# Fetching the chosen rows of one batch by one-hot matmuls from SBUF, in a kernel whose work order a planner writes

## The chip, the cores and the metric

The kernel runs on one core of a Trainium2 chip. The metric is the device time of one launch in microseconds (us), the median of several runs. The profiled execution is one more run, with its own time and a span from the first to the last instruction.

## What is computed

Two parts follow each other. For each of 4 batches, q, k and v are 6208 × 256. An attention across the 256 channels is formed from all 6208 rows, and then 128 rows of its output go through a small two-layer network.

```python
qn = q / (np.linalg.norm(q, axis=1, keepdims=True) + 1e-06)
kn = k / (np.linalg.norm(k, axis=1, keepdims=True) + 1e-06)
s = kn.transpose(0, 2, 1) @ qn / tau
a = softmax(s)                      # 256 x 256 per batch
x = v @ a                           # 6208 x 256 per batch
scores = np.einsum('bsd,d->bs', x, w_gate)
for b in range(4):
    top_idx = the 128 rows with the highest scores[b]
    xe = x[b, top_idx]
    ye = np.maximum(xe @ w1, 0.0) @ w2
    out[b] = x[b]; out[b, top_idx] = xe + sigmoid(scores[b, top_idx])[:, None] * ye
```

## The kernel before

**Tiles.** Each batch is cut into six chunks of 1024 rows and a rest of 64. A chunk lies in SBUF as 128 partitions of 8 rows, so column c of a batch (49 of them) is 128 rows, one to a partition. Loads are issued by POOL (L187, L189) and turn float32 into bfloat16 on the way: first q and k of a batch, then its v. Five buffers hold chunks of q, five of k, five of v; a buffer's next load waits until TensorE has read the old chunk.

**Stages of a batch.** `p1_row` (L292 on) multiplies each row of q and k into the sums of k'q and the squares (L303, L305, L307). `softmax_stages` makes a from them: norms on VectorE, one small matmul (L350), the exponentials (L357, ScalarE), the vector aw = a·w_gate, and a in bfloat16 (L376). `p2_transpose` turns four columns of v at a time on TensorE (L403) into a PSUM bank, and ScalarE (L417) or VectorE (L419) copies them to SBUF as vt_sb; eleven such places exist, and those of batch 3 lie in freed q and k buffers. There are two banks named vt_ps for this, and at the very end also s_ps and g_ps. `p2_score` multiplies turned groups by aw (L440). `p2_out` multiplies two columns at a time by a (L474), here called an output group, and ScalarE evicts each into a stage of float32 (L482), from which SP stores whole chunks (L514).

**Selection.** `select_stages` finds the 128 highest scores: the maxima of each partition are spread over all partitions by a matmul (L544), seven rounds narrow a threshold (compare on VectorE, L557; count on TensorE, L573, and VectorE, L576), then the chosen positions are packed into an index (L587 to L622). POOL gathers the chosen rows of v by an indirect DMA (L626), TensorE turns them (L637), and the attention and the two layers follow (L645 to L689). The result, upd, is scattered over the stored rows by a second indirect DMA from POOL (L721), which waits for the batch's stores. Both DMAs stand in POOL's one queue, between loads.

**Order.** A planner writes the order of every engine when the program is built: at each step it takes the ready piece of work with the best rank, by its own clocks for each engine and a model of the two DMA rings (`Rings`). Its waiting TensorE is kept busy with dead matmuls (`idle`, L865). The number of places for turned groups (`VT_BUFS`) and of load buffers (`V_BUFS`) enters its choices: `in_use`, `limit` and `vt_live` say when a load or a transposition may be placed. So a change of either number changes the order in all batches. Stores of batch 2 and 3 are held back behind the last loads, and two chunks of batch 1 are stored last of all, with their chosen rows already added.

Of the kernel before, what the change touches and what calls it, by code (L numbers as in the profile page):

```python
# [10 lines left out]
F32 = mybir.dt.float32  # L11
BF16 = mybir.dt.bfloat16
# [3 lines left out]
ALU = mybir.AluOpType  # L16
AX = mybir.AxisListType

P = 128
RPP = 8  # L20
CHUNK = RPP * P
NTHR = 8
# [5 lines left out]
def kernel(  # L28
# [12 lines left out]
    nc = tc.nc  # L41

    B, N, C = q.shape
# [7 lines left out]
    NFULL = N // CHUNK  # L51
    REM = N - NFULL * CHUNK
    assert 0 < REM <= P
    NCOL = NFULL * RPP + 1
    inv_tau = 1.0 / float(tau)

    QK_BUFS = 5
    V_BUFS = 5
    ST_BUFS = 9
    VT_BUFS = 11  # L60
    AHEAD = 4

    const = ctx.enter_context(tc.tile_pool(name="const", bufs=1))
# [7 lines left out]
    moe = ctx.enter_context(tc.tile_pool(name="moe", bufs=1))  # L71
# [4 lines left out]
    ps_vt = ctx.enter_context(tc.tile_pool(name="ps_vt", bufs=2, space=PS))  # L76
    ps_o = ctx.enter_context(tc.tile_pool(name="ps_o", bufs=2, space=PS))
    ps_sc = ctx.enter_context(tc.tile_pool(name="ps_sc", bufs=1, space=PS))
    ps_m = ctx.enter_context(tc.tile_pool(name="ps_m", bufs=1, space=PS))
# [3 lines left out]
    v_flat = v.rearrange("b n c -> (b n) c")  # L83
# [65 lines left out]
    rings = Rings()  # L149
    vt_clock = {"pe": 0.8, "dve": 0.8, "act": 0.8, "pool": 0.8, "sp": 0.8}  # L150

    def now():
        return vt_clock["pe"]
# [8 lines left out]
    loaded = {}  # L162
    load_inst = {}
    arrival_key = {}
    in_use = {"qk": 0, "v": 0, "qkr": 0, "vr": 0}
# [3 lines left out]
    dmas = []  # L169
# [94 lines left out]
    for i in range(NSTEP):  # L264
        nc.vector.memset(pows[:, i, :], 1.00001 / (NTHR + 1) ** (i + 1))
    jpows = const.tile([P, NSTEP, NTHR], F32)
    nc.vector.tensor_tensor(out=jpows, in0=pows,
                            in1=iota_row[:, None, 1:NTHR + 1].to_broadcast([P, NSTEP, NTHR]), op=ALU.mult)
    ones_col = const.tile([P, NCOL], BF16)
    nc.vector.memset(ones_col, 1.0)  # L270
    cnt9 = const.tile([P, NTHR + 1], F32)
# [234 lines left out]
    def emit_store(b, ci, parts):  # L506
# [12 lines left out]
        keep.extend(ins)  # L519
        return ins[0]  # L520

    def select_stages(b):
        sc_ps = sc_tiles[b]
        sc = moe.tile([P, NCOL + 1], F32, name="sc")
# [28 lines left out]
        nc.vector.tensor_scalar(out=tab, in0=jpows, scalar1=rng, scalar2=None, op0=ALU.mult)  # L553
        wait = 1.8
        for i in range(NSTEP):
            cmp = moe.tile([P, NCOL, NTHR], BF16, name="cmp", bufs=2)
            nc.vector.scalar_tensor_tensor(out=cmp, in0=sc[:, 0:NCOL, None].to_broadcast([P, NCOL, NTHR]),  # L557
                                           scalar=wl[:, i, NTHR:NTHR + 1],
                                           in1=tab[:, None, i, :].to_broadcast([P, NCOL, NTHR]),
                                           op0=ALU.subtract, op1=ALU.is_ge)  # L560
            if i == 0:
                nc.vector.tensor_scalar(out=wl[:, 0:NSTEP, 0:NTHR], in0=pows, scalar1=rng, scalar2=None,
                                        op0=ALU.mult)
            if i == 1:
                nc.vector.scalar_tensor_tensor(out=slack, in0=wl[:, 0, NTHR:NTHR + 1], scalar=-1.0, in1=top,
                                               op0=ALU.mult, op1=ALU.max)
                nc.vector.tensor_scalar(out=slack, in0=slack, scalar1=-5.0e-7,
                                        scalar2=wl[:, NSTEP - 1, 0:1], op0=ALU.mult, op1=ALU.subtract)
            yield ("pe", 0.2 if i else 0.5, wait, "slot" if i > 1 else "")
            wait = 1.2  # L570
            mps = ps_m.tile([P, 512], F32, name="m_ps")
            for h in range(7):
                nc.tensor.matmul(mps[:, 0:7 * NTHR], lhsT=ones_b,  # L573
                                 rhs=cmp[:, 7 * h:7 * h + 7, :].rearrange("p s j -> p (s j)"),
                                 start=h == 0, stop=h == 6)
            nc.vector.tensor_reduce(out=cnt9[:, 0:NTHR],  # L576
                                    in_=mps[:, 0:7 * NTHR].rearrange("p (s j) -> p j s", s=7),
                                    axis=AX.X, op=ALU.add)
            gej = moe.tile([P, NTHR + 1], F32, name="gej", bufs=2)
            nc.vector.scalar_tensor_tensor(out=gej, in0=cnt9, scalar=float(CAP) - 0.5, in1=wl[:, i, :],  # L580
                                           op0=ALU.is_ge, op1=ALU.mult,
                                           accum_out=wl[:, i + 1, NTHR:NTHR + 1])
# [16 lines left out]
        nc.tensor.matmul(sc_ps[:, 0, 0:1], lhsT=tri_b[:, 0, :], rhs=own_b, start=True, stop=True)  # L599
        excl_b = moe.tile([P, NCOL + 1], BF16, name="excl_b")  # L600
        nc.scalar.copy(excl_b, sc_ps[:, 0, 0:1].to_broadcast([P, NCOL + 1]))
        oh = moe.tile([P, P], BF16, name="oh")
        nc.vector.tensor_scalar(out=oh, in0=iota_row, scalar1=mps[:, 0:1], scalar2=None, op0=ALU.is_ge)
        nc.vector.scalar_tensor_tensor(out=oh, in0=iota_row, scalar=mps[:, 1:2], in1=oh, op0=ALU.is_lt,
# [13 lines left out]
        if b == late[0][0]:  # L618
# [2 lines left out]
        idx = moe.tile([P, 1], I32, name="idx", bufs=2)  # L621
        nc.vector.tensor_scalar(out=idx, in0=tok, scalar1=float(N - 1), scalar2=float(b * N), op0=ALU.min,  # L622
                                op1=ALU.add)
        yield ("pool", 0.15, 0.9)
        vg = moe.tile([P, C], BF16, name="vg", bufs=2)
        ins = nc.gpsimd.indirect_dma_start(out=vg, out_offset=None, in_=v_flat,  # L626
                                     in_offset=bass.IndirectOffsetOnAxis(ap=idx[:, 0:1], axis=0))
        dmas.append(ins)
        vt_clock["pool"] = max(vt_clock["pool"], now()) + 1.0
        rings.add(0, vt_clock["pool"] + 1.0, 0.5, ("gather", b))  # L630
        gathered.add(b)

        yield ("dma", ("gather", b))
        a_sb, _ = a_tiles[b]
        tp = ps_vt.tile([P, 2, 4, P], BF16, name="vt_ps")
        for cc in range(2):
            nc.tensor.transpose(tp[:, cc, 0, :], in_=vg[:, cc * P:(cc + 1) * P], identity=ident_b)  # L637
        vgt = moe.tile([P, 2, P], BF16, name="vgt")
        nc.vector.tensor_copy(vgt, tp[:, :, 0, :])
        yield ("pe", 0.12, 0.3)  # L640

        xt_ps = ps_vt.tile([P, 2, C], F32, name="vt_ps")
        for dc in range(2):
# [88 lines left out]
    def calm():  # L732

        if acc_dead[0]:
            return L in gathered
        if softmaxes[0]:
            return False
        near = eat[eat_at:eat_at + 14]
        return not any(x[0] == "T" for x in near) or near[0][0] == "T"

    class Chain:
# [33 lines left out]
        def ready(self):  # L775
            if self.need[0] == "t":
                if self.b == E and self.mlp and acc_dead[0] and L not in gathered:
                    return FAR
                return self.need[1]
            if self.need[0] == "dma":  # L780
                if self.b < L and not calm() or self.b == L and out_at < len(outs):
                    return FAR

                late_by = vt_clock["pool"] + 3.8 if self.b == L else 0.0
                return max(rings.landing(self.need[1]) + 0.1, late_by)
            b = self.need[1]
            if self.need[0] == "scores":
                return now() if score_at == len(scores) else FAR
            if held[b] or (b >= E and L not in gathered):
                return FAR  # L790
            if b >= E:
                return now()
            return max(rings.landing(key) for key in stored[b]) + 3.0
# [73 lines left out]
    while True:  # L867
# [106 lines left out]
        elif what == "T":  # L974
# [20 lines left out]
            vt_bank = sorted(vt_bank)[1:] + [fin]  # L995
            vt_live = len(from_pool)
            vt_ready[(u[1], g)] = fin
            if eat_at == len(eat) or eat[eat_at][1] != u:
                in_use[bucket(u)] -= 1
        elif what == "S":  # L1000
            b, g = scores[score_at]
# [61 lines left out]
```

## Time and profile before

| | |
|---|---|
| median of 3 runs | 258.37 us (258.06 to 258.6) |
| profiled execution | 257.8 us |
| its span | 255.8 us |
| TensorE busy | 214.7 us (84%) |
| VectorE busy | 92.6 us (36%) |
| ScalarE busy | 106.4 us (42%) |
| POOL busy | 56.9 us (22%) |
| granted TensorE clock, mean | 0.977 |
| read from and written to HBM | 78.91 MB and 25.95 MB |

Times in the profile count from the start of the span. A row of a timeline gives the start, the duration, the engine, the line and the operation, and in square brackets how long its engine had been idle and what released it. PE is TensorE, DVE is VectorE, ACT is ScalarE. A digit of a slice is the busy share in tenths. DMA shares can pass 1 since packets on one engine overlap.

### The profile page before, as it was taken

What the parts mean: (1) busy time and instruction counts of PE and PEld (TensorE: products, weight loads), DVE (VectorE), ACT (ScalarE), POOL (GpSimd) and SP (SyncE); (2) the same over time, 40 slices, a digit from 0 to 9 for tenths busy, and PEclk for the clock granted to TensorE, in tenths of its full rate; (3) what the DMA queues carried; (4) which work ended last, traced back from release to release, by engine and by line L of the source; (5) the groups of instructions that cost most, each with busy time, mean ns of one, the idle gap of its engine ahead of it and who ended that gap; (6) DMA issues with size and microseconds to landing.
All of it is one profiled execution on the core that took longest, in us unless ns stands there. A gap on an engine that the chain in (4) does not pass through costs nothing.

```text
span 255.8 us, 6666 instructions
## 1 busy us (share of the span) xinstructions
PE 214.7 (84%) x2878; PEld 187.9 (73%) x2878; DVE 92.6 (36%) x410; ACT 106.4 (42%) x187; POOL 56.9 (22%) x106
## 2 busy tenths in 40 slices
PE   0099779899998529989999689899999999999962
PEld 0069768798877529879888578788898878887851
DVE  2000002635651003445655006546752064687021
ACT  2800003753564002484244005765313069698740
POOL 7323111422005000622200414212313310000301
PEclk9999999999999959999999999999999999999987
DMA  6999999999999999999999999999999999999995
GB/s 235 259 216 215 213 216 210 215 209 251 274 320 314 316 285 216 218 214 213 249 282 258 213 211 213 215 261 316 220 215 218 212 225 225 407 425 411 404 415 250
DMA packets 17326, 66.87 MB, mean 261 GB/s; under 512 B 2097, under 2 KB 3634, under 8 KB 14450
## 3 DMA queue, kind: packets, MB, share of 16 engines
q0 software_dynamic: 12672, 38.93, 76.5%
q1 hardware_dynamic: 4626, 27.53, 26.7%
q8 instruction: 22, 0.36, 0.5%
q14 instruction: 6, 0.05, 0.0%
HBM read 78.91 MB, written 25.95 MB: 410 GB/s over the span
## 4 chain that ended last, share of the span: by engine, by line
DMA 73%; PE 14%; issue 4%; POOL 4%; DVE 2%; ACT 1%; POOLq 1%; DVEq 0%
DMA k_ch<-in_k_dram 48%; DMA v_ch<-in_v_dram 10%; DMA q_ch<-in_q_dram 10%; DMA out_dram<-stage 4%; PE s_ps L303 2%; PE o_ps L474 2%; PE vt_ps L403 2%; POOL q_ch L187 1%; PE g_ps L307 1%; PE g_ps L305 1%; ACT stage L482 1%; PE s_ps L474 1%; PE sc_ps L440 1%; PE g_ps L474 1%; POOL k_ch L187 1%
## 5 line engine op out<-in xcount | busy, mean ns | idle before, releaser
L303 PE MATMUL s_ps<-q_ch,k_ch 128*128 128x256 bf16 x384 | 90.0, 279 | 28.7 <-DMA k_ch<-in_k_dram 28.7
L305 PE MATMUL g_ps<-q_ch 128*128 128x128 bf16 x384 | 85.5, 223 | 0.0
L307 PE MATMUL g_ps<-k_ch 128*128 128x128 bf16 x384 | 85.5, 223 | 0.0
L482 ACT COPY stage<-o_ps 128x512 f32<-128x512 f32 x77 | 43.9, 589 | 43.6 <-PE o_ps L474 41.6
L303 PEld LDWEIGHTS <-k_ch 128*128 128x128 bf16 x384 | 38.3, 100 | 31.5 <-DMA k_ch<-in_k_dram 30.6
L307 PEld LDWEIGHTS <-k_ch 128*128 128x128 bf16 x384 | 38.3, 100 | 5.2
L305 PEld LDWEIGHTS <-q_ch 128*128 128x128 bf16 x384 | 38.3, 100 | 0.1
L474 PE MATMUL o_ps<-a_sb,vt_sb 128*128 128x256 bf16 (+1 forms) x250 | 35.5, 272 | 1.0 <-ACT stage L482 0.5
L317 DVE CUSTOM_DVE_ANT_0 junk<-g_ps,ident_f 128x128 f32<-128x128 f32 x16 | 4.7, 291 | 66.4 <-PE g_ps L307 66.0
L474 PEld LDWEIGHTS <-vt_sb 128*128 128x128 bf16 (+1 forms) x264 | 23.6, 97 | 6.4 <-issue 3.1
L403 PE MATMUL vt_ps<-ident_b,v_ch 128*128 128x128 bf16 x360 | 25.4, 219 | 2.7 <-ACT vt_sb L417 2.4
L403 PEld LDWEIGHTS <-v_ch 128*128 128x128 bf16 x384 | 23.1, 97 | 5.1 <-issue 3.4
L313 ACT COPY s_sb<-s_ps 128x512 f32<-128x512 f32 x4 | 2.3, 586 | 55.4 <-PE s_ps L303 55.4
L187 POOL DMA_DIRECT2D v_ch<-in_v_dram x26 | 14.2, 545 | 45.8 <-PE vt_ps L403 17.5
L417 ACT COPY vt_sb<-vt_ps 128x1024 bf16<-128x1024 bf16 (+1 forms) x26 | 22.6, 927 | 2.9 <-PE vt_ps L403 2.9
L187 POOL DMA_DIRECT2D q_ch<-in_q_dram x25 | 13.8, 554 | 29.9 <-DMA q_ch<-in_q_dram 10.4
L187 POOL DMA_DIRECT2D k_ch<-in_k_dram x25 | 13.6, 543 | 24.5 <-DMA v_ch<-in_v_dram 10.4
L865 PE MATMUL o_ps<-w_sb,ident_b 128*128 128x256 bf16 x124 | 18.8, 273 | 0.2 <-ACT h_sb L675 0.2
L557 DVE SCALAR_TENSOR_TENSOR cmp<-sc,wl,tab 128x392 bf16<-128x392 f32 x28 | 17.5, 627 | 1.0
L626 POOL DMA_INDIRECT vg<-in_v_dram,idx x4 | 4.0, 1008 | 61.0 <-DVE idx L622 32.8
L865 PEld LDWEIGHTS <-ident_b 128*128 128x128 bf16 x124 | 10.7, 97 | 1.3 <-issue 0.4
L576 DVE TENSOR_REDUCE cnt<-m_ps 128x8 f32<-128x56 f32 x28 | 6.0, 216 | 15.3 <-PE m_ps L573 14.9
(188 smaller groups left out, 273.7 us busy)
## 6 DMA issues: line engine op xcount, KB each, us to landing
out_dram<-stage SPq DMA_DIRECT2D x21, 1024.0 KB, 10.2
q_ch<-in_q_dram POOLq DMA_DIRECT2D x23, 512.0 KB, 17.8
k_ch<-in_k_dram POOLq DMA_DIRECT2D x23, 512.0 KB, 18.5
v_ch<-in_v_dram POOLq DMA_DIRECT2D x22, 512.0 KB, 14.2
stage<-in_moe_w_dram SPq DMA_DIRECT2D x2, 1024.0 KB
out_dram<-stage SPq DMA_DIRECT2D x4, 512.0 KB
v_ch<-in_v_dram POOLq DMA_DIRECT2D x4, 256.0 KB, 12.9
out_dram<-stage SPq DMA_DIRECT2D x2, 384.0 KB, 5.0
```

What stands on the lines that cost most here:

```text
L187: ins = nc.gpsimd.dma_start(out=t[:, rows, :], in_=view(src, b, ci)[:, rows, :])
L303: nc.tensor.matmul(s_ps[:, cc, :], lhsT=ks[:, sl], rhs=qs, start=begin and cc == 0, stop=end and cc == 1)
L305: nc.tensor.matmul(g_ps[:, cc, :], lhsT=qs[:, sl], rhs=qs[:, sl], start=begin and cc == 0, stop=False)
L307: nc.tensor.matmul(g_ps[:, 2 + cc, :], lhsT=ks[:, sl], rhs=ks[:, sl], start=False, stop=end and cc == 1)
L317: nc.vector.tensor_tensor_reduce(out=junk, in0=g_ps[:, i, :], in1=ident_f, scale=1.0, scalar=0.0, op0=ALU.mult, op1=ALU.add, accum_out=nsq ...
L403: nc.tensor.transpose(vt_ps[:, cc, j, :parts], in_=vt[:parts, s0 + j, cc * P:(cc + 1) * P], identity=ident_b[:parts, :parts])
L417: nc.scalar.copy(vt_sb[:, :, :n, :parts], vt_ps[:, :, :n, :parts])
L474: nc.tensor.matmul(o_ps[:parts, pj, :], lhsT=vt_sb[:, cc, j, :parts], rhs=a_sb[:, cc, :], start=pj == 0 and cc == 0, stop=pj == m - 1 and ...
L482: nc.scalar.copy(st[:parts, s0 + pair * 2:s0 + pair * 2 + m, :], o_ps[:parts, :m, :])
L557: nc.vector.scalar_tensor_tensor(out=cmp, in0=sc[:, 0:NCOL, None].to_broadcast([P, NCOL, NTHR]), scalar=wl[:, i, NTHR:NTHR + 1], in1=tab[: ...
L576: nc.vector.tensor_reduce(out=cnt9[:, 0:NTHR], in_=mps[:, 0:7 * NTHR].rearrange("p (s j) -> p j s", s=7), axis=AX.X, op=ALU.add)
L865: nc.tensor.matmul(o_ps[:, 0, :], lhsT=ident_b, rhs=w2_sb[:, 0, :], start=True, stop=True)
```

## The change

For batch 0 alone the gather falls away. The chunks of its v stay in SBUF until the index is known; six buffers hold a whole batch. A new operation gives each chosen element its place (pos), 13 comparisons on VectorE make of it, for every column, a 128 × 128 matrix with a one where a row goes to a place, and TensorE multiplies each column of v by its matrix, summing all 49 columns in one bank. What comes out is already turned, so the two transposes of gathered rows are gone for this batch. A load buffer of v of batch 0 comes free after the picks of its columns instead of after its transposes. V_BUFS goes from 5 to 6, VT_BUFS from 11 to 8, and the gather's tile has one buffer instead of two.

```diff
-    V_BUFS = 5
+    V_BUFS = 6
-    VT_BUFS = 11
+    VT_BUFS = 8
...
+    picked = (0,)
+    GRP = 4
+    place = const.tile([P, P], BF16)
+    nc.vector.tensor_scalar(out=place, in0=iota_row, scalar1=1.0, scalar2=None, op0=ALU.add)
...
+    def pick_rows(b, vp, g, pick):
+        for c in range(g, min(g + GRP, NCOL)):
+            ci, s = (c // RPP, c % RPP) if c < NCOL - 1 else (NFULL, 0)
+            parts = P if ci < NFULL else REM
+            vt = loaded[("v", b, ci)][0]
+            for cc in range(2):
+                nc.tensor.matmul(vp[:, 0, cc * P:(cc + 1) * P], lhsT=vt[:parts, s, cc * P:(cc + 1) * P],
+                                 rhs=pick[:parts, c - g, :], start=c == 0 and cc == 0,
+                                 stop=c == NCOL - 1 and cc == 1)
...
+        if b in picked:
+            pos = moe.tile([P, NCOL], BF16, name="pos")
+            nc.vector.scalar_tensor_tensor(out=pos, in0=pre[:, 0:NCOL], scalar=mps[:, 0:1], in1=msk,
+                                           op0=ALU.add, op1=ALU.mult)
...
+        if b in picked:
+            picks = []
+            for g in range(0, NCOL, GRP):
+                n = min(GRP, NCOL - g)
+                pick = moe.tile([P, GRP * P], BF16, name="cmp", bufs=2).rearrange("p (s t) -> p s t", t=P)
+                nc.vector.tensor_tensor(out=pick[:, 0:n, :], in0=pos[:, g:g + n, None].to_broadcast([P, n, P]),
+                                        in1=place[:, None, :].to_broadcast([P, n, P]), op=ALU.is_equal)
+                picks.append(pick)
+                if g == 0:
+                    yield ("pe", 0.0, 0.6)
+                    vp = ps_m.tile([P, 2, C], F32, name="m_ps")
+                    continue
+                pick_rows(b, vp, g - GRP, picks.pop(0))
+                if g % RPP == 0:
+                    in_use["v"] -= 1
+                yield ("pe", 0.46, 0.3)
+            pick_rows(b, vp, g, picks.pop(0))
+            vgt = moe.tile([P, 2, P], BF16, name="vgt")
+            nc.vector.tensor_copy(vgt, vp[:, 0, :].rearrange("p (a t) -> p a t", a=2))
+            in_use["vr"] -= 1
...
+        else:
+            yield ("pool", 0.15, 0.9)
+            vgt = yield from gathered_rows(b, idx)
...
-            if eat_at == len(eat) or eat[eat_at][1] != u:
+            if (eat_at == len(eat) or eat[eat_at][1] != u) and u[1] not in picked:
                 in_use[bucket(u)] -= 1
```

POOL's queue around the selection of batch 0, before:

```order
L187 DMA q_ch<-in_q_dram 128x2048
L187 DMA k_ch<-in_k_dram 128x2048
L626 DMA vg<-in_v_dram,idx 128x256
L187 DMA q_ch<-in_q_dram 128x2048
L187 DMA k_ch<-in_k_dram 128x2048
L187 DMA v_ch<-in_v_dram 128x2048
L189 DMA v_rem<-in_v_dram 64x256
L187 DMA v_ch<-in_v_dram 128x2048 x2
L721 DMA out_dram<-upd,idx 6208x256
L187 DMA v_ch<-in_v_dram 128x2048 x3
```

The same place in the change:

```order
L187 DMA q_ch<-in_q_dram 128x2048
L187 DMA k_ch<-in_k_dram 128x2048
L187 DMA v_ch<-in_v_dram 128x2048
L189 DMA v_rem<-in_v_dram 64x256
L187 DMA v_ch<-in_v_dram 128x2048 x2
L770 DMA out_dram<-upd,idx 6208x256
L187 DMA v_ch<-in_v_dram 128x2048 x3
```

The gather is gone, and the scatter of batch 0 stands as before after the third v chunk of batch 1.

ScalarE from the exponentials of the last softmax on, before; stage is an eviction of an output group, k_ch and q_ch are places for turned groups of batch 3, in the order of its chunks:

```order
L357 ACTIVATE e,rsum<-e,rn 128x256 x2
L482 COPY stage<-o_ps 128x512
L417 COPY k_ch<-g_ps 128x1024
L417 COPY k_ch<-vt_ps 128x1024
L417 COPY q_ch<-s_ps 128x1024
L417 COPY q_ch<-vt_ps 128x1024
L376 ACTIVATE a_sb<-e,r 128x256 x2
L482 COPY stage<-g_ps 128x512
L482 COPY stage<-o_ps 128x512
L482 COPY stage<-s_ps 128x512
L417 COPY k_ch<-vt_ps 128x1024
```

The same place in the change:

```order
L363 ACTIVATE e,rsum<-e,rn 128x256 x2
L488 COPY stage<-o_ps 128x512
L488 COPY stage<-g_ps 128x512
L423 COPY k_ch<-vt_ps 128x1024
L488 COPY stage<-s_ps 128x512
L488 COPY stage<-o_ps 128x512
L423 COPY k_ch<-g_ps 128x1024
L423 COPY q_ch<-vt_ps 128x1024
L423 COPY q_ch<-s_ps 128x1024
L382 ACTIVATE a_sb<-e,r 128x256 x2
L488 COPY stage<-o_ps 128x512
L488 COPY stage<-g_ps 128x512
```

Three more evictions stand ahead of the copies, and the copy of a later group (k_ch from vt_ps) is VectorE's now. On TensorE (not shown row by row, since eight equal matmuls make a group) four output groups stand where one and 6 dead matmuls stood among the transposes of chunks 1 and 2. The three output groups that stood ahead of the transposes of chunk 3 now stand behind them, ahead of those of chunk 4 and the first half of chunk 5; and before the last half of chunk 5 stand the scores of six groups instead of five.

## Rows read from the trace of the kernel before

**Rows 1.** The page, part 2: busy tenths and GB/s in 40 equal slices.

```profile
DVE  2000002635651003445655006546752064687021
...
DMA  6999999999999999999999999999999999999995
GB/s 235 259 216 215 213 216 210 215 209 251 274 320 314 316 285 216 218 214 213 249 282 258 213 211 213 215 261 316 220 215 218 212 225 225 407 425 411 404 415 250
```

**Rows 2.** Windows of 2 us: length, busy PE, PEld, DVE, ACT, POOL, granted clock, DMA share, GB/s.

```profile
102.00:104.00 2.00, 2.00 (x30) 1.89 (x28) 0.16 (x1) 0.00 (x0) 1.55 (x2) 1.00 1.05 211
...
200.00:202.00 2.00, 2.00 (x31) 1.90 (x29) 0.00 (x0) 0.00 (x0) 0.86 (x2) 1.00 1.14 213
...
224.00:226.00 2.00, 2.00 (x28) 1.51 (x25) 1.57 (x8) 1.82 (x5) 0.00 (x0) 1.00 1.02 430
...
246.00:248.00 2.00, 1.19 (x11) 0.72 (x12) 0.73 (x3) 0.37 (x1) 0.00 (x0) 0.82 1.03 432
```

**Rows 3.** Timeline of POOL: gathers (L626), scatters (L721), loads (L187).

```profile
78.54 1.02 POOL L626 DMA_INDIRECT vg<-in_v_dram,idx  x1 [17.38 <-DVE idx L622]
...
102.44 1.01 POOL L721 DMA_INDIRECT out_dram<-upd,idx  x1 [12.37 <-DVE upd L689]
103.45 1.09 POOL L187 DMA_DIRECT2D v_ch<-in_v_dram  x2
...
236.98 1.01 POOL L626 DMA_INDIRECT vg<-in_v_dram,idx  x1 [28.19 <-DMA out_dram<-stage]
...
251.90 0.97 POOL L721 DMA_INDIRECT out_dram<-upd,idx  x1 [12.59 <-DMA out_dram<-stage]
```

**Rows 4.** Timeline of the end, 236 to 256 us, all engines.

```profile
236.55 0.15 DVE L622 TENSOR_SCALAR idx<-tok 128x1 int32<-128x1 f32 x1
...
246.20 0.29 PE L637 MATMUL vt_ps<-ident_b,vg 128*128 128x128 bf16 x2 [1.52 <-DMA vg<-in_v_dram,idx]
...
251.13 0.48 DVE L689 SCALAR_TENSOR_TENSOR upd<-o_ps,gate,xe 128x256 f32<-128x256 f32 x1 [0.75 <-PE o_ps L684]
```

**Rows 5.** Timeline of PE, 200 to 236 us: chunk 4, last half of chunk 5, maxima.

```profile
216.08 0.61 PE L403 MATMUL vt_ps<-ident_b,v_ch 128*128 128x128 bf16 x8 [0.31 <-DVE k_ch L419]
...
218.96 0.61 PE L403 MATMUL vt_ps<-ident_b,v_ch 128*128 128x128 bf16 x8
...
221.59 0.46 PE L544 MATMUL m_ps<-dmx,ones_f 128*128 128x128 f32 x2
```

**Rows 6.** The page, part 3: packets, MB and share of 16 engines of POOL's queue.

```profile
q0 software_dynamic: 12672, 38.93, 76.5%
```

**Rows 7.** The chain that ended last: start, length, what, how many instructions.

```profile
42.72 0.91 PE vt_ps L403 x16
...
213.46 0.46 PE g_ps L474 x4
...
218.12 0.98 PE sc_ps L440 x40
```

**Rows 8.** Timeline of PE, 82 to 96 us.

```profile
94.28 0.39 PE L303 MATMUL s_ps<-q_ch,k_ch 128*128 128x256 bf16 x1 [6.24 <-DMA k_ch<-in_k_dram]
```

**Rows 9.** Timeline of DVE, 204 to 237 us: the copy of a turned group.

```profile
216.73 0.69 DVE L419 COPY q_ch<-vt_ps 128x1024 bf16<-128x1024 bf16 x1
```

**Rows 10.** The page, part 5: count, busy us, mean ns, idle before.

```profile
L557 DVE SCALAR_TENSOR_TENSOR cmp<-sc,wl,tab 128x392 bf16<-128x392 f32 x28 | 17.5, 627 | 1.0
```

**Rows 11.** Timeline of ACT, 200 to 236 us: evictions (stage) and copies of turned groups.

```profile
210.91 0.56 ACT L482 COPY stage<-o_ps 128x512 f32<-128x512 f32 x1
...
212.28 1.02 ACT L417 COPY k_ch<-vt_ps 128x1024 bf16<-128x1024 bf16 x1
...
214.08 1.04 ACT L417 COPY q_ch<-vt_ps 128x1024 bf16<-128x1024 bf16 x1
...
215.79 0.60 ACT L482 COPY stage<-g_ps 128x512 f32<-128x512 f32 x1
216.26 0.62 ACT L482 COPY stage<-o_ps 128x512 f32<-128x512 f32 x1
```

More of the change, by code (lines that the diff above doesn't have):

```diff
@@ L520, in emit_store, with gathered_rows @@
         return ins[0]
+    def pick_rows(b, vp, g, pick):
[7 more added lines that the diff above has]
+                                 stop=c == NCOL - 1 and cc == 1)
+    def gathered_rows(b, idx):
+        vg = moe.tile([P, C], BF16, name="vg")
+        ins = nc.gpsimd.indirect_dma_start(out=vg, out_offset=None, in_=v_flat,
+                                           in_offset=bass.IndirectOffsetOnAxis(ap=idx[:, 0:1], axis=0))
+        dmas.append(ins)
+        vt_clock["pool"] = max(vt_clock["pool"], now()) + 1.0
+        rings.add(0, vt_clock["pool"] + 1.0, 0.5, ("gather", b))
+        gathered.add(b)
+        yield ("dma", ("gather", b))
+        tp = ps_vt.tile([P, 2, 4, P], BF16, name="vt_ps")
+        for cc in range(2):
+            nc.tensor.transpose(tp[:, cc, 0, :], in_=vg[:, cc * P:(cc + 1) * P], identity=ident_b)
+        vgt = moe.tile([P, 2, P], BF16, name="vgt")
+        nc.vector.tensor_copy(vgt, tp[:, :, 0, :])
+        yield ("pe", 0.12, 0.3)
+        return vgt
     def select_stages(b):
@@ L555, in select_stages @@
         for i in range(NSTEP):
-            cmp = moe.tile([P, NCOL, NTHR], BF16, name="cmp", bufs=2)
+            cmp = moe.tile([P, GRP * P], BF16, name="cmp", bufs=2)[:, 0:NCOL * NTHR].rearrange(
+                "p (s j) -> p s j", s=NCOL)
             nc.vector.scalar_tensor_tensor(out=cmp, in0=sc[:, 0:NCOL, None].to_broadcast([P, NCOL, NTHR]),
@@ L623, in select_stages @@
                                 op1=ALU.add)
[L624 to L633, printed above, removed]
-        a_sb, _ = a_tiles[b]
[L635 to L640, printed above, removed]
+        if b in picked:
[15 more added lines that the diff above has]
+            pick_rows(b, vp, g, picks.pop(0))
+            vgt = moe.tile([P, 2, P], BF16, name="vgt")
+            nc.vector.tensor_copy(vgt, vp[:, 0, :].rearrange("p (a t) -> p a t", a=2))
+            in_use["vr"] -= 1
+            yield ("pe", 0.1, 0.4)
+            yield ("calm",)
+        else:
+            yield ("pool", 0.15, 0.9)
+            vgt = yield from gathered_rows(b, idx)
+        a_sb, _ = a_tiles[b]
         xt_ps = ps_vt.tile([P, 2, C], F32, name="vt_ps")
@@ L779, in ready @@
                 return self.need[1]
+            if self.need[0] == "calm":
+                return now() if calm() else FAR
             if self.need[0] == "dma":
```

## The prediction

> **What bounds the kernel now.** I read the page's forty slices first. The DMA digits are 9 from the second slice to the last but one [rows 1], and the windows of two microseconds say the same: a share of 1.05 to 1.14 while only loads run, at 213 GB/s written (the loads read float32 and write bfloat16, so that is 426 GB/s read), and 1.02 at 430 GB/s while only stores run [rows 2]. So every byte, in either direction, costs the same, and from some 4 us to some 253 us nothing but bytes counts: an engine's saving is worth nothing unless it moves the last bytes or what hangs behind them. What hangs behind them I read in the timeline of the end. The chosen rows of batch 3 are gathered by an instruction that starts at 236.98 [rows 3], 0.28 us after their index is done at 236.70. They are turned at 246.20, go through the two layers, and upd is done at 251.61 [rows 4]. The scatter starts at 251.90 [rows 3] and the span ends at 255.8, 3.9 us later. The scatter's wait is put down to a store, yet upd came only 0.3 us before it. The end is thus a tie of two chains: the byte stream, and the **selection chain** of batch 3, which starts when the last group of v has been turned (218.96) and has its maxima on TensorE at 221.59 [rows 5].
>
> **The change part by part, batch 0.** One gather goes. It writes 128 rows of 512 B, 65.5 KB, and at 213 GB/s that is 0.31 us of the stream [rows 2]. From above: queue 0 took 76.5% of 16 engines' span for 12672 packets, 0.765 × 16 × 255.8 / 12672 = 0.247 us each [rows 6], and 128 such packets on 16 engines are 1.98 us. The mean packet is six times as big as a gathered row, so I take 0.4 us, near the lower end, and keep 0.3 to 2.0. The Trainium skill (DMA: Bandwidth & Descriptors, section Anatomy of one DMA) fits a DMA as about 2.0 us plus its bytes over 436 GB/s, an estimate of 2.2 us here, but lays most of the 2.0 on the receipt of the last write, which other transfers need not wait for; no row shows that split. By its full figure the sum below would be 1.8 us lower.
>
> POOL no longer waits 17.38 us for idx before it can issue the last q and k of batch 1 [rows 3]. Worth nothing: the DMAs were full through that wait. The scatter of batch 0, which POOL still meets at the same place among the v loads, keeps waiting for upd; three v loads stand behind it.
>
> Added on TensorE are 98 matmuls of 128 columns. Sixteen transposes of that size take 0.91 us, 57 ns each [rows 7], so 5.6 us. They lie beside TensorE's waits for k: 6.24 us before 94.28 alone [rows 8]. Added on VectorE are 13 comparisons (12 of 512 numbers). Nearest rows: a copy of 1024 bfloat16 in 0.69 us [rows 9], so 0.35 us for 512 at least, and cmp with 392 numbers in 0.627 us [rows 10], so 0.82 us at most; 4.5 to 10.7 us in slices where VectorE's digits are 1, 0, 0 [rows 1]. I take 0.7 us, nearest to cmp, whose inputs are also repeated along an axis. The Trainium skill (VectorE: DVE Perf Modes, section What auto-detection actually checks) grants two tensors the doubled rate only if all are of 16 bits and step one, which the repeated pos is not; no row here shows this form. With the gain of the gather's two transposes and the copy, cost zero. If that cover were gone, upd of batch 0 would come late, which is rival C.
>
> **Buffers.** A sixth buffer for v lets the sixth v load of each batch go before the first chunk is turned. With DMAs full this only lengthens the queue: zero. v of batch 1 now waits for picks: two of 13 free the first chunk, at some 80 us, where its load stands today anyway; zero. With eight places for v turned in place of eleven, output groups of a batch must come earlier between the transposes. In the first three batches that is hidden behind the stream. In the tail it is not.
>
> **The tail.** Behind the last softmax's small matmul the planner now places four output groups of batch 2 among the first transposes (before: one, and dead work), and the three that stood ahead of chunk 3's transposes now stand between those of chunk 3 and chunk 4. ScalarE has no room there: from 210.91 to 216.88 it evicts and copies without a gap [rows 11]. Step by step from the orders of ScalarE and TensorE shown above, with today's durations:
> - Ahead of the copy that frees the bank for the second half of chunk 3 there were one eviction and four copies; now four evictions and three copies. An eviction costs 0.47 us (215.79 to 216.26) and a copy 0.90 us (half of 212.28 to 214.08) [rows 11]: it ends at 210.91 + 4 × 0.47 + 3 × 0.90 = 215.5, where it ended at 215.0.
> - That half is turned from 215.6 to 216.1, eight scores follow (0.98 us for 40, so 0.2 us), then the three output groups at 0.46 us each [rows 7]: chunk 4 starts at 216.1 + 0.2 + 1.4 = 217.7. Today it starts at 216.08 [rows 5], the groups having come earlier. Its second half takes the other bank at once.
> - The first half of chunk 5 needs the bank of chunk 4's first half: 217.7 + 0.5 + 0.69 for VectorE's copy [rows 9] = 218.9.
> - Before the last half six groups of scores now stand, 1.2 us, where five stood: 218.9 + 0.45 + 1.2 = 220.55, against 218.96 [rows 5]. The slide is **1.6 us**.
>
> From there both orders hold the same work: three output groups and two of scores up to the maxima, and as many output groups in each round of the search. Nothing is lost for ScalarE, since three more outputs are then done; the selection chain merely starts 1.6 us later among them. From below the slide is 0 (the moved groups fill waits), from above 3 × 0.46 + 3 × 0.47 = 2.8 us; I take 1.6, since the steps follow from the orders and only durations are borrowed.
>
> **Sum.** Stream: −0.4. Selection chain: −0.4 + 1.6 = +1.2, of which up to 0.3 us of slack before the scatter swallows 0.2. The end follows the later: **+1.0 us**. The layers of batch 3 run partly at a lower clock (granted 0.82 in 246 to 248, TensorE busy 1.19 of 2 us [rows 2]); a longer wait before them may lower more of it, 0 to 0.6 us; I take 0. The profiled execution took 257.8 us, so 258.8; the median of the runs, 258.37, lies 0.57 above it, so 259.4.
>
> **The rivals.**
> - A, the forecast: 259.4, within 258.9 to 260.3. Chance 0.62.
> - B, not slower: the slide is absorbed. The chain decides only where the slide exceeds the gather's 0.4 plus the slack of 0.2. If the moved evictions find gaps (TensorE waits 0.31 us at 216.08 [rows 5]), the last half is bound by its landing and the whole end moves with the stream: 258.37 − 0.4 = 258.0. Against it speaks ScalarE without gaps. Chance 0.20.
> - C, slower by another way: the load queue runs dry. POOL issues the next v loads at 103.45, behind the scatter at 102.44, with the share still 1.05 [rows 2, 3]. When k of the fifth chunk lands at 94.28 [rows 8], five chunks of 524 KB, 2.46 us each at 213 GB/s, are still queued: full until some 106.6. Were upd later than now by over 2 us (comparisons well over 0.82 us each, in two buffers), every further microsecond costs one: 2 us more, on top of A, 261. Chance 0.08.
> - D, faster: the gather cost the stream the 1.98 us of the upper bound. Then the stream gains 2.0, the chain is at 1.6 − 2.0 − 0.2 = −0.6: 257.8. For it speaks that a small packet may carry a fixed part, against it that the mean packet is six times a gathered row [rows 6]. The full figure of the Trainium skill named above (Anatomy of one DMA) would come out near it. Chance 0.10.
> - That the change doesn't do what it says is excluded by the orders: the gather of batch 0 is gone.
>
> **How the numbers follow.** A measurement of this kernel tells 0.2%, 0.52 us, from no change. Slower by more: A without its lower edge 0.57, C 0.08, 0.65. Within: 0.05 of A, 0.12 of B, 0.03 of D, 0.20. Faster by more: 0.08 of B (a gather at over 0.5 us) and 0.07 of D, 0.15. The range of 257.7 to 260.4 reaches from D to A with a slide of 2.1 and a lower clock; left out are C and the ends.
>
> **What would show it.** Right: three indirect gathers; DMA digits of 9 throughout; the last eight transposes of v at about 220.2 and the last maxima at 222.8; POOL's last scatter at 252.9, waiting for upd and no longer for a store. Wrong: a scatter of batch 3 still behind a store at 251.5 (B), DMA shares under 1 near 105 (C), or the last landing of v over 1 us earlier (D). Late chunks of v or a dearer selection would break the sum.

## The result, and the profile after

The changed kernel took 261.02 us in the median of 6 runs (260.15 to 262.32), the kernel before 258.35 beside it: a ratio of 1.0097, interval 1.0077 to 1.0116. Slower was forecast, by 1.0 us; it is 2.5 by the ratio and 2.7 by the medians. The profiled execution took 261.12 us, its span is 259.4.

The page, parts 2 and 3, answers to [rows 1, 6]:

```profile
DMA  6999999999999999999999999999999999999991
GB/s 246 255 216 214 212 213 211 215 210 282 292 315 313 319 223 214 220 214 196 288 293 214 214 212 213 214 310 272 214 224 208 212 229 290 424 419 394 412 416 53
...
q0 software_dynamic: 12528, 38.87, 75.5%
```

The groups by line have the new comparisons (count, busy us, mean ns, idle before):

```profile
L669 DVE TENSOR_TENSOR cmp<-pos,place 128x512 bf16<-128x512 bf16 x12 | 8.0, 689 | 5.1 <-PE m_ps L534 4.8
```

The stream is as full as before up to the last slice, and that slice is nearly empty (53 GB/s, before 250): the stores are over and something else ends late. One gather is 144 packets (12672 less 12528), and a comparison takes 0.69 us, as forecast.

For the sections to be compared, two rows of TensorE before that were not shown, the last product of k with itself and the small matmul of the last softmax:

```profile
204.78 0.22 PE L307 MATMUL g_ps<-k_ch 128*128 128x128 bf16 x1
...
208.65 0.70 PE L350 MATMUL m_ps<-diag,ones_f 128*128 128x256 f32 x2 [0.39 <-DVE diag L345]
```

The timeline of TensorE after, from the same place to the transposes of batch 3's gathered rows (those of batch 2's stand at 227.98), answers to [rows 4, 5]:

```profile
205.16 0.22 PE L313 MATMUL g_ps<-k_ch 128*128 128x128 bf16 x1
...
209.13 0.60 PE L356 MATMUL m_ps<-diag,ones_f 128*128 128x256 f32 x2
...
212.39 0.61 PE L409 MATMUL g_ps<-ident_b,v_ch 128*128 128x128 bf16 x8 [0.47 <-ACT stage L488]
...
213.79 0.61 PE L409 MATMUL s_ps<-ident_b,v_ch 128*128 128x128 bf16 x8 [0.35 <-ACT stage L488]
...
215.07 0.61 PE L409 MATMUL vt_ps<-ident_b,v_ch 128*128 128x128 bf16 x8
216.46 0.61 PE L409 MATMUL vt_ps<-ident_b,v_ch 128*128 128x128 bf16 x8 [0.78 <-DVE k_ch L425]
...
218.42 1.06 PE L409 MATMUL vt_ps<-ident_b,v_ch 128*128 128x128 bf16 x16
219.81 0.61 PE L409 MATMUL vt_ps<-ident_b,v_ch 128*128 128x128 bf16 x8 [0.34 <-DVE q_ch L425]
...
221.46 0.61 PE L409 MATMUL vt_ps<-ident_b,v_ch 128*128 128x128 bf16 x8
...
224.08 0.46 PE L578 MATMUL m_ps<-dmx,ones_f 128*128 128x128 f32 x2
...
227.98 0.27 PE L550 MATMUL vt_ps<-ident_b,vg 128*128 128x128 bf16 x2
...
249.59 0.39 PE L550 MATMUL vt_ps<-ident_b,vg 128*128 128x128 bf16 x2 [3.73 <-DMA vg<-in_v_dram,idx]
```

The timeline of all engines after, with the scatter of batch 0, then index, gather, upd and scatter of batch 3, answers to [rows 3, 4]:

```profile
102.79 1.03 POOL L770 DMA_INDIRECT out_dram<-upd,idx  x1 [12.80 <-DVE upd L738]
...
239.03 0.15 DVE L661 TENSOR_SCALAR idx<-tok 128x1 int32<-128x1 f32 x1
...
239.96 1.00 POOL L540 DMA_INDIRECT vg<-in_v_dram,idx  x1 [32.87 <-PE o_ps L485]
...
255.10 0.48 DVE L738 SCALAR_TENSOR_TENSOR upd<-o_ps,gate,xe 128x256 f32<-128x256 f32 x1 [1.03 <-PE o_ps L733]
...
255.86 0.97 POOL L770 DMA_INDIRECT out_dram<-upd,idx  x1 [13.60 <-DVE upd L738]
```

Taken from row to row, the two profiles differ so:

| stretch | before | after | difference |
|---|---|---|---|
| last product of k | 204.78 | 205.16 | +0.38 |
| to the small matmul | 3.87 | 3.97 | +0.10 |
| to the last eight transposes of v | 10.31 | 12.33 | **+2.02** |
| to the maxima, then to the index | 17.59 | 17.57 | −0.02 |
| index to gather | 0.43 | 0.93 | **+0.50** |
| gather to its transposes | 9.22 | 9.63 | +0.41 |
| transposes to upd | 4.93 | 5.51 | **+0.58** |
| upd to scatter, then to the end | 4.67 | 4.30 | −0.37 |
| the span | 255.8 | 259.4 | +3.6 |

The three in bold are what the experiments had to explain. Foreseen were the last eight transposes at 220.2, the maxima at 222.8 and the last scatter at 252.9; they came at 221.46, 224.08 and 255.86. Three gathers are left, as foreseen. The span grew by 3.6 us and the medians by 2.7: the profiled execution of the kernel before was 0.57 us faster than its median, so some 0.9 us of the table's sum belongs to the two executions and not to the change. The windows of 2 us answer to the last row of [rows 2] (the granted clock is the third value from the right): TensorE stood for 3.73 us before the transposes, and its clock then fell to 1.2 GHz, half of 2.4.

```profile
248.00:250.00 2.00, 0.39 (x2) 0.23 (x3) 0.00 (x0) 0.00 (x0) 0.00 (x0) 0.76 1.00 408
250.00:252.00 2.00, 1.55 (x12) 1.07 (x12) 0.90 (x3) 0.37 (x1) 0.00 (x0) 0.50 1.06 446
```

### The profile page after: what moved, and what is told of

It reads as the page before. It is cut to its first block, busy times and chain, and to the rows that moved or that the text cites. A ratio compares the mean times of both kernels' runs of the same rounds, so it can differ in the third digit from the quotient of the medians.

```text
span 259.4 us, 6912 instructions
## 1 busy us (share of the span) xinstructions
PE 221.5 (85%) x2972; PEld 194.5 (75%) x2972; DVE 103.7 (40%) x428; ACT 103.6 (40%) x184; POOL 55.7 (21%) x105
## 3 DMA queue, kind: packets, MB, share of 16 engines
q0 software_dynamic: 12528, 38.87, 75.5%
## 4 chain that ended last, share of the span: by engine, by line
PE 42%; DMA 41%; issue 6%; ACT 5%; DVE 4%; POOL 1%; POOLq 1%; DVEq 0%; ACTq 0%
DMA k_ch<-in_k_dram 23%; DMA q_ch<-in_q_dram 9%; PE o_ps L480 8%; PE s_ps L309 7%; PE vt_ps L409 5%; DMA v_ch<-in_v_dram 4%; DMA out_dram<-stage 4%; PE o_ps L916 3%; PE g_ps L313 3%; PE g_ps L311 3%; PE sc_ps L446 3%; PE m_ps L534 2%; ACT stage L488 2%; ACT vt_sb L423 1%; ACT e L363 1%
## 5 line engine op out<-in xcount | busy, mean ns | idle before, releaser
L309 PE MATMUL s_ps<-q_ch,k_ch 128*128 128x256 bf16 x384 | 91.0, 280 | 19.9 <-DMA k_ch<-in_k_dram 19.9
L187 POOL DMA_DIRECT2D v_ch<-in_v_dram x26 | 14.1, 547 | 44.3 <-PE m_ps L534 19.4
L187 POOL DMA_DIRECT2D q_ch<-in_q_dram x25 | 13.7, 548 | 42.6 <-PE g_ps L313 15.3
L423 ACT COPY vt_sb<-vt_ps 128x1024 bf16<-128x1024 bf16 (+1 forms) x24 | 20.9, 921 | 1.6 <-PE vt_ps L409 1.6
L187 POOL DMA_DIRECT2D k_ch<-in_k_dram x25 | 13.5, 539 | 29.3 <-DMA v_ch<-in_v_dram 10.3
L916 PE MATMUL o_ps<-w_sb,ident_b 128*128 128x256 bf16 x122 | 17.1, 273 | 0.2 <-ACT h_sb L724 0.2
L425 DVE COPY vt_sb<-vt_ps 128x1024 bf16<-128x1024 bf16 x11 | 7.6, 691 | 14.4 <-PE vt_ps L409 14.3
L540 POOL DMA_INDIRECT vg<-in_v_dram,idx x3 | 3.0, 997 | 46.0 <-PE o_ps L485 32.9
```

Source lines behind the costliest of these rows:

```text
L187: ins = nc.gpsimd.dma_start(out=t[:, rows, :], in_=view(src, b, ci)[:, rows, :])
L309: nc.tensor.matmul(s_ps[:, cc, :], lhsT=ks[:, sl], rhs=qs, start=begin and cc == 0, stop=end and cc == 1)
L423: nc.scalar.copy(vt_sb[:, :, :n, :parts], vt_ps[:, :, :n, :parts])
L425: nc.vector.tensor_copy(vt_sb[:, :, :n, :parts], vt_ps[:, :, :n, :parts])
L916: nc.tensor.matmul(o_ps[:, 0, :], lhsT=ident_b, rhs=w2_sb[:, 0, :], start=True, stop=True)
```

## The experiments

Theory T: the number of places for v turned makes the planner write another order of the tail, and that order costs the time. Rivals: P, the picks and the buffers they hold; V, eight places are too few elsewhere; G, the single buffer of the gathered rows; C, batch 0's scatter starves the stream.

| run | median, us | ratio to before | interval |
|---|---|---|---|
| the change | 261.02 | 1.0097 | 1.0077 to 1.0116 |
| e1, places alone | 260.58 | 1.0083 | 1.0055 to 1.0111 |
| e2, no batch picked | 260.92 | 1.0120 | 1.0074 to 1.0166 |
| e3, old order of the tail | 259.32 | 1.0037 | 1.0006 to 1.0068 |
| e4, two buffers for gathered rows | 260.09 | 1.0083 | 1.0051 to 1.0115 |
| e5, dead matmuls | 259.66 | 1.0044 | 1.0023 to 1.0066 |
| e6, new order in the kernel before | 259.85 | 1.0056 | 1.0039 to 1.0072 |
| e7, four more gathers | 259.52 | 1.0040 | 1.0026 to 1.0054 |
| e8, three repairs | 258.55 | 1.0003 | 0.9981 to 1.0025 |
| e9, four repairs | 257.59 | 0.9972 | 0.9951 to 0.9994 |
| e10, dead matmuls in the kernel before | 258.26 | 0.9988 | 0.9971 to 1.0005 |
| e11, scatter alone | 260.46 | 1.0082 | 1.0056 to 1.0108 |
| e12, e10 and the scatter | 257.82 | 0.9963 | 0.9943 to 0.9983 |

**e1: places alone** (in the kernel before)

```diff
-    VT_BUFS = 11
+    VT_BUFS = 8
```

> The kernel before with eight places for v turned in place of eleven and nothing else; all four gathers stay, and the gathered rows keep two buffers. The planner then writes the same order behind the last softmax as in the change: four output groups among the transposes of chunk 1, three ahead of chunk 4. Theory T (the order of the tail costs the time): from the small matmul of the last softmax to the last eight transposes some 12.3 us as in the change, not 10.3; +2.0 for that, up to 0.6 more for the layers at the lower clock, 0.2 of slack off: 260.2 to 260.8. Rival P (the picks and the buffers they hold cost it): 258.4, no change. Rival G (the single buffer of the gathered rows is a large part): under 259.5.

Measured 260.58: T's range, with no pick, five buffers and two buffers for gathered rows. P and G do not fit it. So this one number costs, all told, most of what the change costs, but not by the order alone. The slide is even longer, from the small matmul at 208.80 to the last eight at 222.70, 13.9 us:

```profile
208.80 0.60 PE L350 MATMUL m_ps<-diag,ones_f 128*128 128x256 f32 x2
...
222.70 0.61 PE L403 MATMUL vt_ps<-ident_b,v_ch 128*128 128x128 bf16 x8
```

because the clock fell in the midst of it (windows of the same run), which it did not in the change; e6 has the order without that:

```profile
214.00:216.00 2.00, 1.36 (x36) 1.20 (x34) 0.60 (x1) 2.00 (x3) 0.00 (x0) 1.00 1.03 199
216.00:218.00 2.00, 1.86 (x22) 1.55 (x22) 0.78 (x2) 1.44 (x3) 0.00 (x0) 0.61 1.05 283
218.00:220.00 2.00, 2.00 (x15) 1.56 (x13) 0.00 (x0) 1.46 (x3) 0.00 (x0) 0.53 0.95 363
```

**e2: no batch picked** (in the change)

```diff
-    picked = (0,)
+    picked = ()
```

> The change with no batch picked: six buffers for v, eight places, one buffer for the gathered rows, and all four batches gathered. Theory T: as slow as the change or slower by the price of one gather in the stream, 261.0 to 261.6. Rival P (picks cost it): back to 258.4 to 259. What separates this from the change, at the same order of the tail, is what the picks themselves give or take: T expects a difference of 0 to 0.6 us in favour of the picks.

Measured 260.92, 0.1 us under the change and under T's range, far above P's. Without picks the kernel is as slow, but not in the same way: its tail has the lower clock (0.64 and 0.50 in 216 to 220) and a slide of 13.9, where the change has 1.00 and 12.33. So this run alone does not price the picks; e3 and e8, which keep them and lose the time, decide against P.

**e3: the old order of the tail** (in the change; the same frame serves e6, e8 and e9)

```diff
+    script = "O T T T C O T T T T C S S S S O O O T T T S S T T S S S S S T S O S C".split()
...
+        if acc_dead[0] and script:
...
+            able = [a for a in able if a[2] == script[0] or
+                    script[0] == "C" and not isinstance(a[2], str) and a[2].b == L]
```

> The change, picks and all, but behind the last softmax the planner is made to place transposes, scores and output groups in the order of the kernel before. Theory T: the last eight transposes come 10.3 us after the small matmul again, not 12.3; the gather of batch 3 still waits for its single buffer (0.5 us): 258.4 to 259.2. Rival P: the tail is only where the loss shows, and the time stays at 260.5 or above. Rival V (eight places are too few elsewhere): 260 or above.

Measured 259.32, 0.1 above T's range and below that of P and V: the order gives back 1.7 us with picks, buffers and places left as they are. TensorE's rows, small matmul and last eight: 10.63 us apart, 0.30 of it a wait for a landing of v.

```profile
210.07 0.68 PE L356 MATMUL m_ps<-diag,ones_f 128*128 128x256 f32 x2
...
220.70 0.61 PE L409 MATMUL vt_ps<-ident_b,v_ch 128*128 128x128 bf16 x8
```

But the small matmul itself is 1.42 us later than before. A window of this run shows where a part of that arose: right behind batch 0's scatter (103.39 here) the stream thinned out. First the window of the kernel before, then that of e3:

```profile
106.00:108.00 2.00, 2.00 (x24) 1.62 (x21) 1.69 (x12) 1.75 (x3) 1.64 (x4) 1.00 1.07 219
```

```profile
106.00:108.00 2.00, 2.00 (x30) 1.75 (x27) 1.27 (x9) 1.50 (x3) 2.00 (x5) 1.00 0.89 164
```

**e4: two buffers for the gathered rows** (in the change)

```diff
-        vg = moe.tile([P, C], BF16, name="vg")
+        vg = moe.tile([P, C], BF16, name="vg", bufs=2)
```

> The change with two buffers for the gathered rows, as before. Theory T: the gather of batch 3 starts 0.3 us after its index, not 0.8, and the time falls by 0.3 to 0.5 us to 260.5. If the wait of 0.5 us was not the buffer's: 261.0, unchanged.

Index and gather in this run, from the timeline of all engines: 0.43 us apart, as before, where the change has 0.93.

```profile
239.01 0.15 DVE L661 TENSOR_SCALAR idx<-tok 128x1 int32<-128x1 f32 x1
...
239.44 1.00 POOL L540 DMA_INDIRECT vg<-in_v_dram,idx  x1 [32.36 <-DMA out_dram<-stage]
```

So the 0.50 us came with the single buffer. The time alone, 260.09, does not tell it from the change: the intervals overlap.

**e5: dead matmuls**, whose result nothing reads (in the change)

```diff
         yield ("dma", ("gather", b))
+        if b == L:
+            idle(30)
```

> The change with 30 dead matmuls of 256 columns on TensorE ahead of the transposes of batch 3's gathered rows, in the 3.7 us in which TensorE waits for them. If the lower clock (granted 0.76, then 0.50 from 250 us on) costs the layers of batch 3 time, these run at 1.0 now: upd 4.4 to 5.2 us after those transposes instead of 5.99, and the end 0.7 to 1.5 us earlier, 259.5 to 260.3. If the layers are bound by their chain over four engines and not by the clock: 261.0.

Measured 259.66, its interval wholly under the change's. The transposes now stand at 249.23 and upd at 254.13, 4.90 us for 5.51 (to the end of upd, as the expectation counts, 5.38 for 5.99, over the 4.4 to 5.2 expected); the granted clock was 1.00 in 248 to 250, 0.79 in the next window and 0.50 after, so it came down again on the way:

```profile
248.00:250.00 2.00, 0.62 (x7) 0.27 (x5) 0.29 (x1) 0.00 (x0) 0.00 (x0) 1.00 1.03 431
250.00:252.00 2.00, 1.70 (x21) 1.42 (x20) 1.28 (x4) 0.76 (x3) 0.00 (x0) 0.79 0.96 406
```

Not all of the 1.4 us is the clock: in this profile the last eight transposes also stand 0.90 earlier (220.56), with the same slide of 12.4.

**e6: the new order in the kernel before** (the frame of e3, with the change's order)

```diff
+    script = "O T T T C O O T O O T T T C S S S S T T S O O O T T T S S S S S S T S O S C".split()
```

> The kernel before, with eleven places and five buffers of v, in which only the order behind the last softmax is set to that of the change. Theory T: this order alone costs what the eight places cost, 259.9 to 260.7. Rival V (the places cost the time elsewhere): 258.4.

Measured 259.85, just under T's range: with eleven places, five buffers and all gathers, the order by itself costs 1.5 us (interval 1.0 to 1.9). V falls. TensorE's rows are 12.07 us apart:

```profile
209.48 0.70 PE L350 MATMUL m_ps<-diag,ones_f 128*128 128x256 f32 x2 [0.39 <-DVE diag L345]
...
221.55 0.61 PE L403 MATMUL vt_ps<-ident_b,v_ch 128*128 128x128 bf16 x8
```

**e7: four more gathers** (in the kernel before, of batch 0's rows, read by nobody)

```diff
+            for i in range(4):
+                nc.gpsimd.indirect_dma_start(out=spare[:, i * C:(i + 1) * C], out_offset=None, in_=v_flat,
+                                             in_offset=bass.IndirectOffsetOnAxis(ap=idx[:, 0:1], axis=0))
```

> The kernel before, with four more gathers behind the gather of batch 0, of the same rows, to a tile that nobody reads before it is written anew. It prices a gather in the stream: at the lower bound of 0.31 us each +1.2 us, 259.6; at the 0.4 that the forecast took +1.6, 260.0; at the upper bound of 1.98 +7.9, 266.3. At zero, 258.4.

Measured +0.40% (0.26 to 0.54): 1.03 us for four, **0.26 us a gather** (0.17 to 0.35). That is about the 0.31 us of its bytes; the upper bound of 1.98 is out.

**e8: three repairs** (in the change: e3, e4 and 26 dead matmuls)

```diff
+        if b == L:
+            idle(26)
```

> The change with three repairs: the tail in the order of before, two buffers for the gathered rows, and 26 dead matmuls ahead of the transposes of batch 3's gathered rows. Theory T: the chain of batch 3 is as early as before or earlier, and the byte stream sets the end: 258.0 to 258.9, level with the kernel before or up to 0.4 us faster by the gather that is gone. If the picks cost the stream something of their own: 259 or above.

Measured 258.55, inside T's range and no difference from the kernel before: the three repairs undo the whole loss, with the picks in place. The layers now run at the full clock. In the timeline of all engines the transposes stand at 248.38 and upd 3.58 us later, where before they took 4.93; below it, the window of 250 to 252.

```profile
248.38 0.28 PE L552 MATMUL vt_ps<-ident_b,vg 128*128 128x128 bf16 x2
...
251.96 0.48 DVE L740 SCALAR_TENSOR_TENSOR upd<-o_ps,gate,xe 128x256 f32<-128x256 f32 x1 [0.23 <-PE o_ps L735]
```

```profile
250.00:252.00 2.00, 1.92 (x24) 1.35 (x24) 1.55 (x7) 0.91 (x4) 0.00 (x0) 1.00 1.01 426
```

TensorE came to the transposes without a wait, 10.37 us after the gather where it was 9.22 before, so the dead work may have held them up. The runs spread from 257.42 to 259.79, and in the profile, of one that took 259.18, the stream is thinner again at 106 us (GB/s 186, share 1.00).

**e9: four repairs** (e8 with 16 dead matmuls, and batch 0's scatter placed behind the last v load of batch 1)

```diff
+            if b == 0 and nxt_unit[0] <= units.index(("v", 1, LAST)):
+                return FAR
```

> The kernel with the three repairs (old tail, two buffers, 16 dead matmuls now), and POOL's scatter of batch 0 set behind the last three v loads of batch 1 instead of ahead of them. In two profiles with picks the DMA share fell to 1.00 and 0.97 near 106 us, right behind that scatter, which waits for upd until 103.4 us. If the load queue runs dry there (theory C), the share stays at 1.05 from 104 to 110, the last product of q and k ends up to 1 us earlier, and the median falls to 257.5 to 258.1, under the kernel before. If not: 258.5, unchanged.

Measured 257.59, in C's range: faster than the kernel before by 0.06 to 0.49%. The share at that place is whole:

```profile
106.00:108.00 2.00, 2.00 (x33) 1.92 (x31) 1.07 (x7) 1.26 (x2) 0.82 (x2) 1.00 1.05 211
```

The last product of k stands at 204.50, in e8 at 205.14. But two things differ from e8, the scatter and the number of dead matmuls, and the intervals of e8 and e9 overlap.

**e10: dead matmuls in the kernel before** (10 of them, at the place of e5)

```diff
+        if b == L:
+            idle(10)
```

> The kernel before with 10 dead matmuls ahead of the transposes of batch 3's gathered rows, where TensorE waits 1.52 us. Theory T (the selection chain and the stores end level in the kernel before): the layers run 1.3 us faster at the full clock, but the scatter then waits for the last store, and the end moves by 0 to 0.4 us: 258.0 to 258.4. If the chain alone set the end: 257.0 to 257.4.

Measured 0.9988, inside T's range and not told from no change, though upd follows the transposes after 3.58 us (247.78 to 251.36) in place of 4.93. The profiled execution, the longest of twelve (259.02), shows where that gain went: its last product of k stands at 205.63, 0.85 later than before, and from the scatter (252.13) to the end it took 5.0 us where it took 3.9. The stores still ran (share 0.95 in 252 to 254, before 0.59), and the stream set the end.

**e11: the scatter alone** (the edit of e9 in the change)

> The change with nothing altered but the place of batch 0's scatter: behind the last three v loads of batch 1. Theory C (the late scatter starves the stream): up to 1 us faster than the change, 260.0 to 260.6. Theory T alone: 261.0, since the profile of the change shows a share of 1.06 there.

Measured 260.46, inside C's range, yet the intervals of this run and of the change overlap. The last product of k stands at 204.31, 0.85 earlier than in the change. But in e5, whose scatter stands where the change's does, it stands at 204.21, and in both the scatter itself started some 1 us earlier than in the change (101.81 and 101.72 for 102.79). Inconclusive by time and by the profile.

**e12: e10 and the scatter** (in the kernel before: the scatter of batch 0 two v loads later)

```diff
+            if b == 0 and nxt_unit[0] <= units.index(("v", 1, order[-2])):
+                return FAR
```

> The kernel before with the 10 dead matmuls and with the scatter of batch 0 one v load later in POOL's queue: the repairs that helped the change, without its picks. If the repairs alone make the faster version, 257.4 to 257.9, level with it. If the kernel before was never starved behind that scatter (its share there is 1.05 or more) and the picks' missing gather is what is left: 258.0 to 258.4.

Measured 0.9963, and 257.82 is inside the range of the repairs alone: level with e9, without any pick. (The edit sets two v loads ahead of the scatter, issued at 94.39 and 95.15, not one.) The kernel before took 258.80 beside it and 258.40 in the other comparisons; against 258.40 the gain is 0.2%. So the repairs are enough for what made e9 fast; of the gather that the picks save, the medians tell nothing. Its chain is 1.35 us earlier than before, but the span is the same, 255.8, 5.1 us behind the scatter: here the stream sets the end.

```profile
249.78 0.48 DVE L691 SCALAR_TENSOR_TENSOR upd<-o_ps,gate,xe 128x256 f32<-128x256 f32 x1 [0.23 <-PE o_ps L686]
...
250.69 0.98 POOL L723 DMA_INDIRECT out_dram<-upd,idx  x1 [11.45 <-DMA out_dram<-stage]
```

```profile
106.00:108.00 2.00, 2.00 (x29) 1.73 (x27) 1.35 (x9) 1.60 (x3) 0.33 (x1) 1.00 1.08 217
```

## Why the prediction was right in its sign and too small

The order of the tail cost what it was said to cost, and more was lost in terms that the sum had at nothing or with the wrong sign. In the two profiles the span grew by 3.6 us where +1.0 was forecast. The 2.6 between them are the stream (0.78), the clock of the layers (0.58), the second buffer of the gathered rows (0.50), the tail (0.42), the slack (0.2) and 0.1 of the rest.

**The bound** (two chains that end level): right in the main. The change made the selection chain late, and the last slice of the stream went empty; in e12 the chain came early, and the stream set the end.

**The tail, +1.6.** The mechanism was right: e1 and e6 make the loss without the picks, e3 takes it away with them. The size was 2.02, and the step of the slide that failed is the second half of chunk 3. Counted from the small matmul, I had it at 6.95 us (215.6 less 208.65); it came at 7.33 (216.46 less 209.13). I had taken ScalarE's copy as the one that frees its bank. That copy ended about when I said (215.5 and the 0.48 by which the small matmul is later make 215.98; it was 214.99 and 1.06, 216.05), but the trace lays the wait on VectorE's copy of chunk 3's first half (rows of ScalarE, then of VectorE):

```profile
214.99 1.06 ACT L423 COPY q_ch<-vt_ps 128x1024 bf16<-128x1024 bf16 x1
```

```profile
215.72 0.69 DVE L425 COPY k_ch<-vt_ps 128x1024 bf16<-128x1024 bf16 x1 [2.90 <-PE vt_ps L409]
```

In the program as it is built, both halves of chunk 3 lie in the same one of the two vt_ps banks, so the second half waits until the first is turned and copied out. That first half was turned at 215.07, behind two waits of TensorE for evictions, 0.47 and 0.35 us (rows of 212.39 and 213.79), which I had not counted. In e6, which has the same order, the two halves lie in two banks. There the second half does wait for ScalarE's copy, and comes 7.08 us after the small matmul:

```profile
216.56 0.61 PE L403 MATMUL vt_ps<-ident_b,v_ch 128*128 128x128 bf16 x8 [0.21 <-ACT q_ch L417]
```

The slide of e6 is 1.76 us, near the 1.6, so by estimate 0.26 of the missing 0.42 goes with the shared bank. Behind this step every distance is within 0.2 us of the forecast's: 9.29 for chunk 4 (9.05 forecast), 10.68 (10.25) and 12.33 (11.9), with the 0.38 of this step in each.

**Slack of 0.2 before the last scatter: wrong.** In the change, with the stores over, the scatter still starts 0.28 us after upd, as it did before after 0.29. That stretch is its start, not a wait for stores. The profile's label in [rows 3] named a store, and I believed it. Only in e12 is the stretch longer, 0.43, with a store named.

**The stream, −0.4.** The price of a gather was sized nearly right (0.26). But the last product came 0.38 later, not 0.4 earlier. I had said that the scatter of batch 0 bites only if upd came over 2 us late, and that margin was too wide. Where the scatter stood ahead of the three v loads and started at 103.32 to 103.49 (e6, e3, e10, e8; before 102.44), the share in 106 to 108 was 0.99, 0.89, 1.00 and 1.00. Where it started by 102.83 (before, the change, e4, e5) it was 1.04 to 1.08, and so it was in e9 and e12, where v loads stood ahead of a scatter at 103.63 and 103.75. (e7, with four more gathers in the queue, has 1.04 at 103.24.) So upd 0.9 us late already bites, with picks (e3, e8) or without (e6, e10). In e3 the window moved 164 GB/s where loads alone move 213, by estimate 0.46 us. Rival C was thus no rival but a part of the sum, in some executions. I had also put the first v load of batch 1 at some 80 us; the picks held it back to 84.45 (80.64 before). But the last load ahead of the scatter was issued at 89.46 (89.55 before), so that the same loads were in the queue.

The 0.38 of the change's own profile is not of this kind: its share there is 1.08. Its low stretch is at 122 to 123 us, 143 GB/s at a share of 1.07, where the kernel before moved 213; it is the slice of 196 in the page. e3, e4 and e8 have such a stretch, the kernel before, e6 and e10 have one at 124 to 126, and e5, e9 and e11 have none. In these three the last product stands at 204.21, 204.50 and 204.31, 0.28 to 0.57 earlier than before, as the −0.4 would have it. What makes the stretch is open.

**Buffers at zero.** The section on the change names the gathered rows' second buffer as gone, and I priced nothing. It cost 0.50 us on the last chain (e4). The label of the gather's row, PE o_ps, misleads: the transposes that read the buffer last stand at 227.98, 12 us earlier. From index to gather it is 0.93 us in all five profiles with one buffer and 0.43 in all nine with two. In the program as it is built, the gather with one buffer has a wait for those transposes as well, and the wait for the index stands on an instruction of its own ahead of it. Why that takes 0.50 us no run separates.

**The clock at zero, of 0 to 0.6.** It cost 0.58 in the profile: I took the lower end without a reason, and it was the upper one. e5 gives it back (4.90 us for 5.51), and e8 shows that even the kernel before paid: at 1.00 the layers take 3.58 us, so 1.35 less. The Trainium skill (TensorE: Matmul & The Clock Gate, Part 1) says that the low rate is the default and that activity releases it. The rows of e8 agree: granted 1.00 in 250 to 252 behind the dead work, where the change has 0.50 behind its wait.

**Picks hidden: right**, as far as the medians tell. 13 comparisons of 0.69 us and 98 matmuls cost nothing that e8 against the kernel before, or e9 against e12, can tell.

Left open are the 0.41 us that the last gather's transfer took longer. The 0.37 that the end took less goes with the stores: where they were over when the last scatter started (the change, e1, e2, e4, e5, e6, e11) the end followed it after 3.4 to 3.6 us, and where they still ran (the other seven) after 3.9 to 5.1.

## What to carry to other kernels

In a kernel whose order a planner writes, a buffer count is an edit of the order: compare the last chain's rows before and after, and price every wait in it, that of a buffer taken away too. Two repairs of what the change laid bare, dead work before a wait and a scatter behind more of the loads, made the kernel before faster by 0.2 to 0.6% with nothing of the change in it. And if an instruction starts the same 0.3 us after its last operand in run after run, that is a start-up time and no slack, whatever releaser the profile names.

## What was not expected of the hardware

The same order of the tail ran at a granted clock of 1.00 in the change, e4, e5, e6 and e11, and at 0.61 and 0.53 in e1 and 0.64 and 0.50 in e2 (216 to 218 and 218 to 220), which cost some 1.6 us (13.9 for 12.33). What TensorE did in the 2 us before does not tell them apart: it was busy 1.36 us in e1 and 1.68 in e2, and 1.68 in the change and 1.22 in e5. And a gather of 128 rows took 0.26 us of a full stream. The Trainium skill (DMA: Bandwidth & Descriptors, Anatomy of one DMA) has figures that make 2.2 us, an estimate, of such a DMA by itself; e7 shows nothing of a fixed part in the stream's time.
